# Attention backward with shared K and V heads on one core: whole-batch transfers in ten row slots, and a new order of all units

## The chip, the cores and the metric

One core of a Trainium2 chip runs the kernel alone. The metric is the device time of one execution in microseconds (us). Engines: PE does matrix products and transposes, ACT, DVE and POOL work on tiles, SP issues all the transfers of this kernel, and 16 DMA engines move the bytes. Tiles lie in SBUF with 128 partitions; PE writes to PSUM, here 8 banks of 128 x 512 fp32.

## The reference

Forward attention and its gradients for 32 batches, 32 query heads with 4 query rows each, 4 K/V heads of 2048 rows, head size 128, all in bf16. Eight query heads share one K/V head, so a batch has 4 groups of 32 query rows, 128 rows in all. Per batch:

```
S = q k^T * scale          P = softmax(S)           O = P v
dV = P^T dO                dP = dO v^T              dS = P * (dP - rowsum(O * dO))
dQ = dS k * scale          dK = dS^T q * scale
```

Outputs are O, dQ, dK and dV. q, dO, O and dQ are 32 KB per batch each; K, V, dK and dV are 2 MB per batch each, so a batch moves about 8.5 MB and the whole call 272.65 MB.

## The kernel before, in words

The host lays K and V out as rows: partition p of a batch holds, for each head, 2048 bf16 values. A pair of heads is one row of 4096 values (8192 B, `ROW`). The first pair's K row carries q behind it and the second pair's carries dO (4224 values, 8448 B, `LONG`); dV's and dK's second rows carry O and dQ in the same way. So a batch is loaded with four transfers of 128 rows, about 1 MB each (LK0, LK1, LV0, LV1; line 226), and stored with four (SV0, SV1, SK0, SK1; line 320). `SLOTS = 20` row buffers in SBUF hold loads and results alike: a slot goes from a loaded row to a result row and back. Batch 0 is loaded in halves of a row.

There is no loop over batches that fixes the order. The string `PLAN` lists every unit of work of all batches in the order in which it is emitted, four characters each: the unit's name (through `NAMES`), its part, where it goes (a PSUM bank, an engine A or D, or a slot) and a buffer number. `plan()` reads it, `emit(u)` writes the unit's instructions. Each engine runs its own units in that order; semaphores are set where one unit needs another's data or buffer.

The units of a batch b, with their lines:

- KT, VT (241): one half of one head's K or V block transposed on PE, as fp32 pairs, 4 transposes of 128 x 128 into one bank; KTe, VTe (207 on ACT, 209 on DVE) copy the bank to SBUF. QT and QTe do the same for q and dO.
- S (255): scores, 2 x 8 products into banks 4 to 7. MX (260): negated maximum on DVE. EX (264): exponential on ACT, with its sum. RC, dop, qp, rs: the reciprocal of the sum and dO and q scaled by it.
- ET, ETe, O, Oe (241, 288, 296): the exponentials transposed, O, and O scaled. DL (299): rowsum of O and dO.
- DV, DVe (310, 316): dV in eight parts of 128 x 1024, each evicted as bf16 into a result row by ACT or DVE.
- DP (255), DS (303): dP and dS in two halves. DT, DTe, DQ, DQe: dS transposed, dQ, and dQ scaled. DK, DKe (310, 316): dK in eight parts like dV.

From batch 10 or so the order repeats every batch. Beside batch b's softmax, O and dV stand the K transposes of batch b+1 and the rest of dQ and dK of batch b-1; O of b and dQ of b-1 stand close together. SP's part of a period is SK0(b-1), LV1(b+2), LK0(b+3), SK1(b-1), SV1(b), LV0(b+2), SV0(b), LK1(b+3). SP runs its transfers in that order and waits at each for its slot and its data.

Of the kernel before, what the change touches and what calls it, by code (L numbers as in the profile page):

```python
# [16 lines left out]
ROW = 2 * 16 * P  # L17
LONG = ROW + P
BANKS = 8
SLOTS, E_TILES, DS_TILES = 20, 2, 2  # L20
# [8 lines left out]
    "a000a110b120a030b040a150e400f4A0e011f0A0e702f7A0e513f5A0b160a070e224f2A0e135f1D0c000d0D0e316f3A0g720h7A0e637f6A0"  # L29
    "b080a190g601h6D0g212h2A0i040i1-0j0D0g303h3A0e411f4A0e024f0A0g104h1D0k0A0g415h4D0g026h0D0l0D0e705f7A0e516p020q0A0"  # L30
    "f5D0b1a0p131q1D0m0-0A340B3A0A060B0D0A100B1A0a0d0r020r1-0s0D0t0D0o0-0A640B6A0A760B7D0u020v0D0g502h5A0A540B5A0E1c0"
    "b0e0A460B4A0e210f2D0e102f1D0c020d0D0e333f3A0A240B2A0E0b0u160v1D0g703h7A0e617f6A0n0-0C020D0D0C140D1A0C360D3D0a1h0"
    "g604h6A0g216h2A0i021i1-0j0D0C200D2A0g360h3A0e470f4A0w100x1A0k0A0g111h1D0g462h4D0g075h0D0C400D4D0w061x0A0l0D0e072"
    "f0A0C620D6A0F0f0C740D7D0e763f7A0e504p010q0A0f5D0b1i0p171q1D0m0-0A320B3A0A040B0D0A100B1A0a040r060r1-0s0D0t0D0A720"
    "B7D0o0-0A640B6A0u061v0D0g500h5A0y010C540D5A0y1-0z0D0F1g0A520B5A0E120b0c0A460e201f2A0B4D0e115f1D0c040d0D0e356f3A0"
    "A220B2A0E0j0u160v1D0g701h7A0e617f6A0n0-0C040D0D0C120D1A0C360D3D0a180g605h6A0g216h2A0i020i1-0j0D0C200D2A0g360h3A0"
    "e471f4A0w101x1A0g112h1D0k0A0g463h4D0g074h0D0C400D4D0w060x0A0l0D0e072f0A0C620D6A0F060C740D7D0e765f7A0e506p010q0A0"
    "f5D0b100p171q1D0m0-0A320B3A0A040B0D0A100B1A0a0g0r060r1-0s0D0t0D0o0-0A620B6A0A740B7D0y070C500D5A0y1-0z0D0F1b0u020"
    "v0D0g560h5A0A540B5A0E1f0b020A400B4D0e270f2A0e163f1A0c020d0D0e334f3D0A240B2A0E010u100v1D0g722h7A0e637f6A0n0-0C060"
    "D0D0C140D1A0C300D3D0a130g624h6A0g236h2A0i041i1-0j0D0C220D2A0g300h3A0C720e410f4A0w100x1A0g111h1D0k0A0g403h4D0g015"  # L40
    "h0D0C440D4A0w001x0D0l0D0D7A0e012f0D0C660D6A0F0a0e743f7D0e504p020q0A0f5D0b150p111q1D0m0-0A340B3A0A060B0D0A120B1A0"
    "a0b0r000r1-0s0D0t0D0o0-0A640B6A0A760B7D0y010C520D5A0y1-0z0D0F1j0u041v0D0g500h5A0A560B5A0E160b0f0A420B4D0e211f2A0"
    "e105f1A0c040d0D0e356f3D0A260B2A0E0e0u120v1D0g711h7A0e607f6A0n0-0C040D0D0C160D1A0C320D3D0a170g615h6A0g206h2A0i040"
    "i1-0j0D0C200D2A0g320h3A0e431f4A0w101x1A0g112h1D0k0A0g423h4D0g034h0D0C400D4D0w020x0A0l0D0e032f0A0C640D6A0F0i0C760"
    "D7D0e725f7A0e506p010q0A0f5D0b190p131q1D0m0-0A340B3A0A060B0D0A100B1A0a0j0r020r1-0s0D0t0D0o0-0A640B6A0A760B7D0y030"
    "C500D5A0y1-0z0D0F110u040v0D0g520h5A0A560B5A0E1a0b060A400B4D0e230f2A0e123f1A0c040d0D0e354f3D0A260B2A0E0c0u100v1D0"
    "g732h7A0e627f6A0n0-0C040D0D0C160D1A0C300D3D0a1h0g634h6A0g226h2A0i041i1-0j0D0C220D2A0g300h3A0e410f4A0w120x1A0g131"
    "h1D0k0A0g403h4D0g015h0D0C420D4D0w001x0A0l0D0e012f0A0C640D6A0F000C760D7D0e703f7A0e514p020q0A0f5D0b1e0p131q1D0m0-0"
    "A340B3A0A060B0D0A100B1A0a010r020r1-0s0D0t0D0o0-0A640B6A0A760B7D0y030C500D5A0y1-0z0D0F1d0u041v0D0g520h5A0A560B5A0"
    "E1i0b0a0A400B4D0e231f2A0e125f1A0c040d0D0e356f3D0A260B2A0E020u100v1D0g731h7A0e627f6A0n0-0C040D0D0C160D1A0C300D3D0"  # L50
    "a180g635h6A0g226h2A0i040i1-0j0D0C220D2A0g300h3A0e411f4A0w121x1A0g132h1D0k0A0g403h4D0g014h0D0C420D4D0w000x0A0l0D0"
    "e012f0A0C640D6A0F050C760D7D0e705f7A0e516p020q0A0f5D0b1f0p131q1D0m0-0A340B3A0A060B0D0A100B1A0a0d0r020r1-0s0D0t0D0"
    "o0-0A640B6A0A760B7D0y030C500D5A0y1-0z0D0F140u040v0D0g520h5A0A560B5A0E100b090A400B4D0e230f2A0e123f1A0c040d0D0e354"
    "f3D0A260B2A0E0c0u100v1D0g732h7A0e627f6A0n0-0C040D0D0C160D1A0C300D3D0a1g0g634h6A0g226h2A0i041i1-0j0D0C220D2A0g300"
    "h3A0e410f4A0w120x1A0g131h1D0k0A0g403h4D0g015h0D0C420D4D0w001x0A0l0D0e012f0A0C640D6A0F0i0C760D7D0e703f7A0e514p020"
    "q0A0f5D0b160p131q1D0m0-0A340B3A0A060B0D0A100B1A0a040r020r1-0s0D0t0D0o0-0A640B6A0A760B7D0y030C500D5A0y1-0z0D0F130"
    "u041v0D0g520h5A0A560B5A0E150b0e0A400B4D0e231f2A0e125f1A0c040d0D0e356f3D0A260B2A0E020u100v1D0g731h7A0e627f6A0n0-0"
    "C040D0D0C160D1A0C300D3D0a1b0g635h6A0g226h2A0i040i1-0j0D0C220D2A0g300h3A0e411f4A0w121x1A0g132h1D0k0A0g403h4D0g014"
    "h0D0C420D4D0w000x0A0l0D0e012f0A0C640D6A0F000C760D7D0e705f7A0e516p020q0A0f5D0b1a0p131q1D0m0-0A340B3A0A060B0D0A100"
    "B1A0a030r020r1-0s0D0t0D0o0-0A640B6A0A760B7D0y030C500D5A0y1-0z0D0F170u040v0D0g520h5A0A560B5A0E1i0b0f0A400B4D0e230"  # L60
    "f2A0e123f1A0c040d0D0e354f3D0A260B2A0E0c0u100v1D0g732h7A0e627f6A0n0-0C040D0D0C160D1A0C300D3D0a190g634h6A0g226h2A0"
    "i041i1-0j0D0C220D2A0g300h3A0e410f4A0w120x1A0g131h1D0k0A0g403h4D0g015h0D0C420D4D0w001x0A0l0D0e012f0A0C640D6A0F0h0"
    "C760D7D0e703f7A0e514p020q0A0f5D0b150p131q1D0m0-0A340B3A0A060B0D0A100B1A0a070r020r1-0s0D0t0D0o0-0A640B6A0A760B7D0"
    "y030C500D5A0y1-0z0D0F1j0u041v0D0g520h5A0A560B5A0E100b060A400B4D0e231f2A0e125f1A0c040d0D0e356f3D0A260B2A0E020u100"
    "v1D0g731h7A0e627f6A0n0-0C040D0D0C160D1A0C300D3D0a1e0g635h6A0g226h2A0i040i1-0j0D0C220D2A0g300h3A0e411f4A0w121x1A0"
    "g132h1D0k0A0g403h4D0g014h0D0C420D4D0w000x0A0l0D0e012f0A0C640D6A0F010C760D7D0e705f7A0e516p020q0A0f5D0b1i0p131q1D0"
    "m0-0A340B3A0A060B0D0A100B1A0a0j0r020r1-0s0D0t0D0o0-0A640B6A0A760B7D0y030C500D5A0y1-0z0D0F180u040v0D0g520h5A0A560"
    "B5A0E1h0b0a0A400B4D0e230f2A0e123f1A0c040d0D0e354f3D0A260B2A0E0c0u100v1D0g732h7A0e627f6A0n0-0C040D0D0C160D1A0C300"
    "D3D0a1f0g634h6A0g226h2A0i041i1-0j0D0C220D2A0g300h3A0e410f4A0w120x1A0g131h1D0k0A0g403h4D0g015h0D0C420D4D0w001x0A0"
    "l0D0e012f0A0C640D6A0F0d0C760D7D0e703f7A0e514p020q0A0f5D0b100p131q1D0m0-0A340B3A0A060B0D0A100B1A0a080r020r1-0s0D0"  # L70
    "t0D0o0-0A640B6A0A760B7D0y030C500D5A0y1-0z0D0F1g0u041v0D0g520h5A0A560B5A0E110b050A400B4D0e231f2A0e125f1A0c040d0D0"
    "e356f3D0A260B2A0E020u100v1D0g731h7A0e627f6A0n0-0C040D0D0C160D1A0C300D3D0a160g635h6A0g226h2A0i040i1-0j0D0C220D2A0"
    "g300h3A0e411f4A0w121x1A0g132h1D0k0A0g403h4D0g014h0D0C420D4D0w000x0A0l0D0e012f0A0C640D6A0F040C760D7D0e705f7A0e516"
    "p020q0A0f5D0b1h0p131q1D0m0-0A340B3A0A060B0D0A100B1A0a0g0r020r1-0s0D0t0D0o0-0A640B6A0A760B7D0y030C500D5A0y1-0z0D0"
    "F1b0u040v0D0g520h5A0A560B5A0E1d0b0i0A400B4D0e230f2A0e123f1A0c040d0D0e354f3D0A260B2A0E0c0u100v1D0g732h7A0e627f6A0"
    "n0-0C040D0D0C160D1A0C300D3D0a1a0g634h6A0g226h2A0i041i1-0j0D0C220D2A0g300h3A0e410f4A0w120x1A0g131h1D0k0A0g403h4D0"
    "g015h0D0C420D4D0w001x0A0l0D0e012f0A0C640D6A0F030C760D7D0e703f7A0e514p020q0A0f5D0b110p131q1D0m0-0A340B3A0A060B0D0"
    "A100B1A0a0b0r020r1-0s0D0t0D0o0-0A640B6A0A760B7D0y030C500D5A0y1-0z0D0F190u041v0D0g520h5A0A560B5A0E140b000A400B4D0"
    "e231f2A0e125f1A0c040d0D0e356f3D0A260B2A0E020u100v1D0g731h7A0e627f6A0n0-0C040D0D0C160D1A0C300D3D0a150g635h6A0g226"
    "h2A0i040i1-0j0D0C220D2A0g300h3A0e411f4A0w121x1A0g132h1D0k0A0g403h4D0g014h0D0C420D4D0w000x0A0l0D0e012f0A0C640D6A0"  # L80
    "F070C760D7D0e705f7A0e516p020q0A0f5D0b1d0p131q1D0m0-0A340B3A0A060B0D0A100B1A0a090r020r1-0s0D0t0D0o0-0A640B6A0A760"
    "B7D0y030C500D5A0y1-0z0D0F1e0u040v0D0g520h5A0A560B5A0E130b0h0A400B4D0e230f2A0e123f1A0c040d0D0e354f3D0A260B2A0E0c0"
    "u100v1D0g732h7A0e627f6A0n0-0C040D0D0C160D1A0C300D3D0a1i0g634h6A0g226h2A0i041i1-0j0D0C220D2A0g300h3A0e410f4A0w120"
    "x1A0g131h1D0k0A0g403h4D0g015h0D0C420D4D0w001x0A0l0D0e012f0A0C640D6A0F0f0C760D7D0e703f7A0e514p020q0A0f5D0b140p131"
# [64 lines left out]
def plan():  # L149
    text, seen, units = "".join(PLAN), collections.Counter(), []  # L150
    for at in range(0, len(text), 4):
        key = text[at:at + 2]
        u = Unit()
        u.name, u.part, u.b = NAMES[key[0]], int(key[1]), seen[key]
        u.where, u.tile = text[at + 2], int(text[at + 3], 36)
        seen[key] += 1
        units.append(u)
# [204 lines left out]
```

## Time and profile before

| what | value |
|---|---|
| timed runs | 671.26, 671.86, 672.22 us; median 671.86 us |
| the profiled execution: span from first to last instruction | 671.1 us |
| median of the timed runs less that span | 0.76 us |
| mean granted PE clock | 0.982 |
| HBM read, written | 136.31, 136.31 MB |
| 1024 KB loads of V, 1056 KB loads of K: median from issue to landing | 20.5, 18.1 us |
| stores of 1056 and 1024 KB: median from issue to landing | 20.1, 20.4 us |
| chain of waits by engine | DMA 50%, PE 37%, DVE 4%, ACT 4%, issue 3% |

How to read the profile. Busy time is given for each engine, with its share of the span. Further rows cut the span into 40 equal slices of 16.8 us: digits are tenths of a slice, PEclk is the clock that PE was granted, and the GB/s row tells what the DMA engines moved. A packet is what one DMA engine moves at a time; here one row of a transfer is one packet. The queue q1 carries the kernel's transfers, q8 and q14 those of instructions. The chain of waits goes back from the last instruction to what released it, step by step; a table by stage gives every engine's busy time in a stretch that one chooses.

### The profile page before, as it was taken

To read this page: it belongs to the slowest core of one execution; us is meant where nothing else is said; L and a number is where in the kernel's file an instruction comes from. 1 tells how busy PE (TensorE), PEld (TensorE's weight loads), DVE (VectorE), ACT (ScalarE), POOL (GpSimd) and SP (SyncE) were. 2 spreads that over 40 slices of the span, in tenths; PEclk is the share of its full clock that TensorE was granted. 3 is DMA by queue.
4 is the path that set the end of the run, shared out by engine and by line. 5 is a ranking of instruction groups with operands and counts; after the bars stand their busy time and mean duration, and the time that the engine had idled before them with its cause. 6 is when DMAs were issued, how large, how long until landed. Compare 5 with 4: busy or idle time off the path is not lost.

```text
span 671.1 us, 20678 instructions
## 1 busy us (share of the span) xinstructions
PE 607.9 (91%) x8768; PEld 401.4 (60%) x8768; DVE 572.0 (85%) x736; ACT 569.6 (85%) x802; POOL 39.0 (6%) x102
## 2 busy tenths in 40 slices
PE   6998999999998999988998989988999989898993
PEld 5665566666665666655655655655655666565651
DVE  1988799999997999988888989887888979896994
ACT  4997899999997999888888989887888979886894
POOL 0000000000000000000000000000000000000000
PEclk9999999999998999999999999998999989998997
DMA  9999999999999999999999999999999999999867
GB/s 354 417 424 423 419 381 423 423 423 423 423 426 424 424 423 424 424 425 426 414 420 425 413 417 421 414 422 424 396 388 408 417 424 424 404 421 423 347 258 322
DMA packets 37533, 273.97 MB, mean 408 GB/s; under 512 B 4160, under 2 KB 4160, under 8 KB 5184
## 3 DMA queue, kind: packets, MB, share of 16 engines
q1 hardware_dynamic: 37440, 272.65, 98.2%
q8 instruction: 69, 1.13, 0.6%
q14 instruction: 24, 0.20, 0.1%
HBM read 136.31 MB, written 136.31 MB: 406 GB/s over the span
## 4 chain that ended last, share of the span: by engine, by line
DMA 50%; PE 37%; DVE 4%; ACT 4%; issue 3%; SPq 0%; POOL 0%; DVEq 0%; ACTq 0%; POOLq 0%
DMA row<-in_k_dram 50%; PE psum L241 19%; PE psum L310 8%; PE psum L288 5%; PE psum L255 5%; ACT row L316 3%; DVE vt_sb L209 2%; DVE ds_sb L303 1%; DVE row L316 0%; DVE e_sb L260 0%; ACT e_sb L264 0%; PE psum L230 0%; SPq L226 0%; ACT dt_sb L207 0%; DVE row L296 0%
## 5 line engine op out<-in xcount | busy, mean ns | idle before, releaser
L241 PE MATMUL psum<-ident,row 128*128 128x128 f32 x2048 | 290.1, 284 | 28.4 <-DMA row<-in_k_dram 21.5
L316 ACT CAST row<-psum 128x1024 bf16<-128x1024 f32 x292 | 289.2, 1023 | 30.9 <-PE psum L310 29.1
L241 PEld LDWEIGHTS psum<-ident,row 128*128 128x128 f32 x2048 | 224.7, 143 | 94.8 <-issue 32.0
L316 DVE CAST row<-psum 128x1024 bf16<-128x1024 f32 x220 | 264.9, 1217 | 5.7 <-PE psum L310 2.9
L207 ACT COPY kt_sb<-psum 128x512 f32<-128x512 f32 x190 | 110.2, 598 | 20.6 <-PE psum L241 20.4
L207 ACT COPY vt_sb<-psum 128x512 f32<-128x512 f32 x160 | 92.0, 602 | 35.3 <-PE psum L241 34.6
L303 DVE SCALAR_TENSOR_TENSOR ds_sb<-psum,delta,e_sb 128x1024 bf16<-128x1024 f32 x64 | 82.1, 1283 | 13.4 <-PE psum L255 9.0
L310 PE MATMUL psum<-ds_sb,qp_sb 32*128 32x512 bf16 x512 | 76.9, 383 | 3.4 <-ACT row L316 1.0
L260 DVE TENSOR_SCALAR_CACHE_REDUCE e_sb<-psum 128x2048 bf16<-128x2048 f32 x32 | 73.3, 2292 | 5.7 <-PE psum L255 5.7
L310 PE MATMUL psum<-e_sb,dop_sb 32*128 32x512 bf16 x512 | 68.8, 388 | 2.5 <-issue 1.0
L209 DVE COPY kt_sb<-psum 128x1024 bf16<-128x1024 bf16 x66 | 45.0, 685 | 28.4 <-PE psum L241 27.8
L209 DVE COPY vt_sb<-psum 128x1024 bf16<-128x1024 bf16 x96 | 60.7, 684 | 10.0 <-PE psum L241 9.8
L264 ACT ACTIVATE e_sb<-psum,m 128x2048 bf16<-128x2048 f32 x32 | 64.0, 2001 | 0.2 <-DVE e_sb L260 0.2
L271 POOL TENSOR_SCALAR dop_sb<-row,rinv 128x128 bf16<-128x128 bf16 x32 | 19.3, 603 | 605.3 <-DVE rinv L268 530.3
L241 PE MATMUL psum<-ident,ds_sb 128*128 128x128 f32 x256 | 41.8, 286 | 9.6 <-DVE vt_sb L209 7.0
L288 PE MATMUL psum<-row,dt_sb 128*32 128x128 bf16 x2048 | 43.5, 222 | 6.2 <-issue 5.6
L310 PEld LDWEIGHTS <-qp_sb 32*128 32x128 bf16 x512 | 19.4, 91 | 46.1 <-issue 42.6
L255 PE MATMUL psum<-vt_sb,qdt_sb 128*32 128x512 bf16 x512 | 40.7, 388 | 4.6 <-issue 4.5
L288 PEld LDWEIGHTS <-dt_sb 128*32 128x32 bf16 x2048 | 30.8, 95 | 22.0 <-issue 21.1
L241 PEld LDWEIGHTS psum<-ident,ds_sb 128*128 128x128 f32 x256 | 26.9, 140 | 27.2 <-DVE vt_sb L209 16.4
L207 ACT COPY dt_sb<-psum 128x512 f32<-128x512 f32 x63 | 38.4, 611 | 1.0 <-PE psum L241 0.9
L288 PEld LDWEIGHTS <-et_sb 128*32 128x32 bf16 x2048 | 30.4, 95 | 13.8 <-ACT et_sb L207 11.3
(29 smaller groups left out, 310.1 us busy)
## 6 DMA issues: line engine op xcount, KB each, us to landing
out_dram<-row SPq DMA_DIRECT2D x64, 1056.0 KB, 20.1
out_dram<-row SPq DMA_DIRECT2D x64, 1024.0 KB, 20.4
row<-in_k_dram SPq DMA_DIRECT2D x62, 1056.0 KB, 18.1
row<-in_v_dram SPq DMA_DIRECT2D x62, 1024.0 KB, 20.5
row<-in_v_dram SPq DMA_DIRECT2D x4, 512.0 KB, 9.4
row<-in_k_dram SPq DMA_DIRECT2D x2, 544.0 KB, 5.3
row<-in_k_dram SPq DMA_DIRECT2D x2, 512.0 KB, 4.4
```

Of the source, the lines that this page charges most:

```text
L207: nc.scalar.copy(out=out.bitcast(FP32), in_=in_)
L209: nc.vector.tensor_copy(out=out, in_=in_.bitcast(BF16))
L241: nc.tensor.transpose(out=ps[:, P * j:P * j + P], in_=src[:, 4 * half + j, :], identity=ident32[:])
L255: nc.tensor.matmul(out[r, QW * w:QW * w + QW], lhsT=t["qdt"][:, P * side + 32 * h:P * side + 32 * h + 32], rhs=t[x, NH * i + h][:, QW * w: ...
L260: nc.vector.tensor_scalar(out=t["e"][:], in0=t["S"], scalar1=-scale, scalar2=None, op0=ALU.mult, op1=ALU.min, accum_out=t["m"][:])
L264: nc.scalar.activation(out=t["e"][:], in_=t["S"], func=ACT.Exp, bias=t["m"][:], scale=scale, accum_out=t["l"][:])
L271: nc.gpsimd.tensor_scalar(out=t["dop"][:], in0=t["go"], scalar1=t["rinv"][:], scalar2=None, op0=ALU.mult)
L288: nc.tensor.matmul(t[name][r, :], lhsT=left[:, j, r, odd], rhs=right[:, 4 * i + j, :, odd], start=(i == 0 and c == 0), stop=(i == 1 and c ...
L303: nc.vector.scalar_tensor_tensor(out=t["ds"][:, w], in0=t["DP", i], scalar=t["dl"][:], in1=t["e"][:, w], op0=ALU.subtract, op1=ALU.mult)
L310: nc.tensor.matmul(acc[:, QW * (h % 2):QW * (h % 2) + QW], lhsT=t[still][rows[h], :], rhs=t[moving][rows[h], QW * i:QW * i + QW], start=Tr ...
L316: copy(out=heads_of(t[name[:2], "out", g])[:, :, QW * i:QW * i + QW], in_=t[name[:2], i, g].rearrange("p (h c) -> p h c", h=2))
```

## The change

Rows become whole batches. K, V, dK and dV of a batch are one transfer each: 128 rows of 16384 B, K with q and dO behind it (16896 B), dK and dV with dQ and O behind them (16640 B). Ten slots of 16896 B replace twenty of 8448 B; the bytes in SBUF are the same. Batch 0's K and V are loaded in four pieces, and batch 31's dV and dK are stored in two. The host packs accordingly.

`PLAN` is written anew: the same kinds of units and the same work, in another order. SP's part of a period is SK(b-2), LV(b+2), LK(b+3), SV(b). The rest of a period in the new order, cut to the units about O and dQ:

```
before: ... DV1(b) O(b) Oe DL DV6 DV7 DQ(b-1) DK5(b-1) DQe DP0(b) DS0 VT5 DV5 ... DP1(b) DS1 ...
after:  ... DV3(b) O(b) Oe DV7 DV1 DV6 KT5(b+1) DV5 VT5(b) DK5(b-1) DL DP0(b) DQ(b-1) DV2 DV4 ... DP1(b) DQe DS1 ...
```

In a period the PSUM evictions of line 316 go from 9 on ACT and 7 on DVE to 10 and 6; the copies of KT, VT, ET and DT from 14 on ACT and 6 on DVE to 13 and 7; DQe goes from DVE to ACT. In the repeating part V(b+2) takes the slot that dV(b-1) had, K(b+3) that of V(b), dV(b+1) that of dK(b-2), and dK(b) that of K(b-1).

```diff
-ROW = 2 * 16 * P
-LONG = ROW + P
+ROW = 4 * 16 * P
+OUT, LONG = ROW + P, ROW + 2 * P
...
-SLOTS, E_TILES, DS_TILES = 20, 2, 2
+SLOTS, E_TILES, DS_TILES = 10, 2, 2
+WHOLE = 9
...
-            x = slots[int(u.where, 36)]
-            for h in range(2):
-                t[name[1], 2 * i + h] = x[:, Sk * h:Sk * h + Sk]
+            x, n, src = slots[int(u.where, 36)], *((LONG, k_r) if name == "LK" else (ROW, v_r))
+            for h in range(NH):
+                t[name[1], h] = x[:, Sk * h:Sk * h + Sk]
             if name == "LK":
-                t["q" if i == 0 else "go"] = x[:, ROW:LONG]
-            n = LONG if name == "LK" else ROW
-            src = (k_r if name == "LK" else v_r)[i][b]
-            for w in (slice(0, Sk), slice(Sk, n)) if b == 0 else (slice(0, n),):
-                nc.sync.dma_start(out=x[:, w], in_=src[:, w])
+                t["q"], t["go"] = x[:, ROW:ROW + P], x[:, ROW + P:LONG]
+            cuts = [0, n] if i == WHOLE else [2 * Sk * i, 2 * Sk * i + Sk, n if i else 2 * Sk]
+            for w in map(slice, cuts, cuts[1:]):
+                nc.sync.dma_start(out=x[:, w], in_=src[b][:, w])
...
-            n = LONG if i else ROW
-            nc.sync.dma_start(out=(dv_r if name == "SV" else dk_r)[i][b], in_=t["D" + name[1], "out", i][:, 0:n])
+            w = slice(0 if i in (0, WHOLE) else ROW // 2, OUT if i else ROW // 2)
+            nc.sync.dma_start(out=(dv_r if name == "SV" else dk_r)[b][:, w], in_=t["D" + name[1], "out"][:, w])
```

## The prediction

> **What bounds the kernel now.** I read the page's DMA rows first, since the sum of traffic is fixed, then the table by stage, then the chain of waits, then SP's own queue.
>
> ```profile
> span 671.1 us, 20678 instructions
> PE 607.9 (91%) x8768; PEld 401.4 (60%) x8768; DVE 572.0 (85%) x736; ACT 569.6 (85%) x802; POOL 39.0 (6%) x102
> ...
> DMA  9999999999999999999999999999999999999867
> GB/s 354 417 424 423 419 381 423 423 423 423 423 426 424 424 423 424 424 425 426 414 420 425 413 417 421 414 422 424 396 388 408 417 424 424 404 421 423 347 258 322
> DMA packets 37533, 273.97 MB, mean 408 GB/s; under 512 B 4160, under 2 KB 4160, under 8 KB 5184
> ...
> q1 hardware_dynamic: 37440, 272.65, 98.2%
> q8 instruction: 69, 1.13, 0.6%
> ```
>
> The 16 DMA engines are full in 37 of 40 slices, at about 424 GB/s; only the last three (from 620 us on) are open. 272.65 MB at 424 GB/s are 643 us of the 671.1. Of the rest, the last slices and a few slow ones (381, 396, 388) hold nearly all. The 4160 packets under 512 B are 260 DMAs times 16 engines: each DMA ends with one 4-byte packet on each engine. The table by stage (stretch: length, busy time of PE, PEld, DVE, ACT, POOL, clock, DMA share, GB/s):
>
> ```profile
> 121.85:140.70 18.85, 18.50 (x279) 12.21 (x282) 17.84 (x24) 17.54 (x26) 1.20 (x3) 1.00 1.01 425
> ```
> ```profile
> 399.60:420.10 20.50, 18.60 (x274) 12.29 (x274) 17.99 (x24) 17.71 (x25) 1.29 (x5) 1.00 1.01 421
> ```
> ```profile
> 631.25:671.10 39.85, 28.52 (x515) 16.48 (x513) 28.25 (x36) 29.11 (x39) 1.39 (x4) 0.91 0.71 289
> ```
>
> The first two are one batch each. Early, compute runs a batch in 18.85 us, PE busy for 18.5 of them, and eats the lead that the first loads gave it; later a batch takes 20.5 us with PE idle for 1.9: there the DMA queue paces it. The chain of waits says the same in time order: from 255 us to 606 us it is nearly all DMA, in pieces of one batch.
>
> ```profile
> 399.63 20.42 DMA row<-in_k_dram
> 420.12 20.46 DMA row<-in_k_dram
> ```
>
> The third stretch is the tail. The last load has landed, only stores are left, each waits for compute, and the engines are busy for 0.71 of it: 39.85 x 0.71 = 28.3 us. About 1.55 us lie after the last packet, so some **10.0 us are gaps** in which the queue had nothing to send.
>
> **The price of a row.** The trace keeps a record of each packet. Medians on one engine: 4096 B 159 ns, 4352 B 168, 8192 B 309, 8448 B 319, the 4-byte packet 9. In the full stretches each starts 3 to 4 ns before the last one's recorded end, so consecutive DMAs land 1.25 us apart (512 KB), 2.45 (1024 KB) and 2.53 (1056 KB). Two landings of 512 KB are 2.50 us, one of 1024 KB is 2.45: merging two DMAs into one with rows twice as long saved about 0.047 us (unrounded). By the recorded durations without the overlap it is 2 x 159 - 309 = 9 ns a row, for 8 rows an engine, and one 9 ns packet: 0.081 us.
>
> **The change, part by part.**
>
> 1. Transfers. Bytes stay the same (K rows 16896 B, V 16384, dK and dV 16640). 260 DMAs become 134: 126 x 0.047 = 5.9 us less of full DMA time; by the other count 126 x 0.081 = 10.2. No q1 row is that long, so from the other side: the nearest row of that size is the instruction page, 69 packets of 16 KB in 0.6% of 16 x 671.1 us, some 934 ns each. It shares its engine with q1; less one row of 309 ns between, 625 ns, against 2 x 305.8 = 611.6 for two rows now. 32 batches x 4 tensors x 8 rows = 1024 rows an engine x 13.4 ns is 13.7 us more. So -10.2 to +13.7; I take -5.9, because the four q1 sizes lie on one line and are the nearer rows.
>
> 2. The tail. Before, SP has issued the last load at 619 us and 11 stores follow it, most waiting for data. After, the last load (V of batch 31) stands behind the store of dK(27); after it come dV(29), dK(28), dV(30), dK(29), dV(31), dK(30), dK(31), seven transfers of 4.93 us. Let x be the moment at which dK(26) lands and releases the slot for dV(29), 0.41 of the way through batch 29's units. From x the queue holds five more transfers, 24.6 us, then the seven, 34.5 us: full until x + 59. Compute, no longer held, starts the scores of batch 31 1.59 batches later, x + 30.5 at 19.2 us a batch, and by the trace of before the last eviction is 20.5 us behind those: x + 51. The last store of dK (in two halves) has its place from x + 54. dV(31)'s first half is ready about x + 44, its place x + 44.3; dK(30) x + 46, place x + 47. So the queue stays fed, with 0 to 3 us to spare: of the 10.0 us of gaps I keep 1, bounds 0 and 5. **-9.0 us.**
>
> 3. The start. K(1) whole now precedes the lower half of V(0), which lands about 2.4 us later (18.2 us, not 15.7). The transposes that need it are after the first exponential, which ends at 19.7 in the trace of before; so 0 to 2 us for compute, and nothing for the queue: six loads fill it until 33 us, and the dV(0) store that is next needs dV(0), ready at 28.3 before. Cover gone, that wait would be a gap of as much.
>
> 4. The slots. Ten whole ones replace twenty halves, the same memory, freed later. In the period SP issues dK(b-2), V(b+2), K(b+3), dV(b). V(b+2) goes where dV(b-1) was, so SP is held until that store lands, with K(b+3), dV(b) and dK(b-1) queued behind it in that order. Cover: the store of dK(b-2), 4.93 us. K(b+3) waits for the last read of V(b), at 0.62 of batch b, over a batch earlier. dV(b+1) goes where dK(b-2) was: that landing is now what holds compute. Semaphore waits on landings were there before too (SP, for its DMAs' landings, in the waits view), so I cost these at 0; what they cost uncovered is the slower rival below.
>
> 5. The order of the units. PE does the same work, 18.5 us a batch. Per batch ACT gets one PSUM eviction more (+1.02), one 128x512 copy less (-0.60) and the scaling of dQ (0.35): 17.5 to 18.3. DVE goes from 17.8 to 17.0. Score matmuls (1.05), minimum (2.29), exponential (2.00) and their hand-overs make a chain of 5.9 us; in it the new order gives PE those matmuls (0.9), eight transposed blocks (8 x 0.43) and a dK pair (0.3): 4.7. So PE may wait 1.2 us: 18.85 at best, 18.5 + 1.2 = 19.7 at worst; placing the units one after the other with these durations I get 19.2. All are under the queue's 20.3, so the order costs 0. It decides only from 19.9 on: the scores of batch 1 start at 30.4 us and those of batch 31 28.6 us before the end (chain of waits), so 30.4 + 30 x 19.9 + 28.6 = 656.
>
> **Sum.** 671.1 - 5.9 - 9.0 = 656.2 of span. The median of the runs shown (671.86) is 0.76 above the span, so 657.0. Counting up from packets instead (2 us before the first, 632 us of rows, 12.4 us by which packets ran over their medians, 4.7 us of instruction fetch, 1.6 us at the end, 1 of gaps, 0.8) gives 654.5. I take **656.0**.
>
> Two rules weighed. The trace's landings, 2.45 us apart for 1024 KB, hold no fixed cost beyond the 0.047 above. The Trainium skill's DMA: Bandwidth & Descriptors (Anatomy of one DMA) gives about 2.0 us fixed plus bytes over 436 GB/s for each DMA; 126 fewer would then be 252 us, an estimate, if none of it were hidden; eight DMAs in flight (20 us to land, 2.5 apart) hide it here. The same page (Queues, rings and completion order) speaks against the change: an engine drains a whole packet of one queue before it turns to another, so an instruction page would wait behind rows of 0.61 us (by the line through the sizes above), not 0.31. An estimate by it is 69 x 0.3 = 21 us if every page stalled an engine; the chain of waits has 3% of issue time in all, and that is covered while the queue paces.
>
> **Rivals.**
> - Compute paces (chance 0.12). The new order runs at 20.0 to 20.3 us a batch, because ACT at 18.3 and PE at 18.5 get in each other's way. For it: PE is busy for 18.5 of 18.85 already. Against: the sums in 5. 30.4 + 30 x 20.15 + 28.6 = 663.5; 659 to 668.
> - The long rows bring nothing or cost (0.08). Rows at 625 ns: +13.7 instead of -5.9, and the tail as forecast: 671.1 + 13.7 - 9.0 + 0.8 = 676.6 at the far end, 663 with no gain at all. For it: the only 16 KB packets are slow; against: those share their engine.
> - Slower: SP starves the queue (0.10). At each V load SP waits for a landing with one transfer, 4.93 us, as cover. The landing is that of the slowest engine (one DMA's landings are up to 2.5 us apart here), then an issue (0.34 us) and about 1.0 us from issue to packet, as at the start: 3.9 us. From 4.93 on it decides. Past it by 1.0 us for 28 batches: 656 + 28 = 684. At 0.6 us it is 673. For it: eight DMAs in flight become two at that moment; against: 1.0 us of margin.
> - The forecast: the queue full from 2 us to nearly the end, 650 to 660 (0.70).
>
> The range takes the forecast, compute pacing and the rows without gain: 648 to 669, leaving the 684 and 677 cases and a run that loses the slow packets too (about 0.17). Under 0.2% (1.3 us) can't be told from no change here. Faster 0.84, within 0.2% 0.03, slower 0.13.
>
> **What would show it.** q1 with 19552 packets, 2144 under 512 B; middle slices at 427 to 429 GB/s; a batch of the paced part at about 20.2 us; DMA digits at 9 to the last slice or two. Median issue to landing: V loads near 10 us, K 15, dV 20, dK 25. Records of 16384 B near 609 ns; 625 would be the second rival. DMA digits of 7 or 8 in the middle would be starving; PE at 9 throughout with the DMA open, compute pacing. A tail at 0.7 of DMA share would prove step 2 wrong.

## The result, and the profile after

The changed kernel is slower: 688.71 us median (four runs, 686.49 to 688.98) against 672.04 for the kernel before (four runs beside it). The ratio is 1.0241, 95% interval 1.0224 to 1.0258. The forecast was 656.0, faster. The rival that gave the slower side, "SP starves the queue", had a chance of 0.10, and 684 us at 1.0 us a batch. The median is 2.5 us above the profiled span; the prediction had added 0.8.

The page of the changed kernel, rows that answer to those of before:

```profile
span 686.2 us, 20449 instructions
...
DMA  9999999999999999999999999999999999999996
GB/s 362 419 426 426 426 426 357 409 409 382 430 424 423 400 390 388 393 371 408 397 405 398 391 429 380 398 389 406 414 394 400 411 392 406 387 401 407 378 422 289
DMA packets 19674, 273.93 MB, mean 399 GB/s; under 512 B 2176, under 2 KB 2176, under 8 KB 3200
...
q1 hardware_dynamic: 19584, 272.64, 97.9%
```

Every DMA digit is a 9, to the last slice but one: the tail is as full as forecast. But a full digit isn't a full rate. From the 14th slice on (223 us) the queue moves mostly 370 to 414 GB/s where 427 to 429 were forecast. I had named digits of 7 or 8 in the middle as the sign of starving, and this page has none; the sign stands one row lower. The table by stage shows it more sharply (stretch: length, busy time of PE, PEld, DVE, ACT, POOL, clock, DMA share, GB/s). First the changed kernel:

```profile
275.50:295.14 19.64, 19.12 (x276) 12.68 (x275) 17.10 (x22) 18.41 (x27) 1.20 (x3) 1.00 1.00 399
441.00:462.70 21.70, 21.11 (x300) 13.62 (x298) 18.29 (x24) 20.41 (x30) 1.20 (x3) 1.00 0.99 393
517.20:521.00 3.80, 3.61 (x88) 2.23 (x88) 3.57 (x6) 3.80 (x6) 0.00 (x0) 1.00 1.02 322
646.40:686.20 39.80, 24.96 (x354) 14.79 (x354) 21.72 (x26) 24.52 (x33) 1.21 (x3) 0.79 0.87 366
```

In all four stretches the engines are busy for 0.87 to 1.02 of the time, yet 322 to 399 GB/s come out: packets take longer than their medians. The third stretch is the second half of one K load. The chain of waits in the middle is made of pieces that end in stores, not in K loads as before (start, length, what):

```profile
530.87 25.57 DMA out_dram<-row
...
573.43 20.75 DMA out_dram<-row
595.59 25.11 DMA out_dram<-row
```

And SP's own waits name the wait that the change added. The first line is the load's wait for a store in the kernel before (line 226); the other two are the changed kernel's (line 217 is the load, line 311 the store):

```profile
SPq L226 <- DMA out_dram<-row: 105.4, 23, 5.6
```

```profile
SPq L217 <- DMA out_dram<-row: 449.3, 27, 19.9
SPq L311 <- DVE row L307: 79.1, 12, 19.1
```

For 449 us, in 27 pieces, SP stands at a load (nearly always V's) and waits for a store to land; before it was 105 us in 23 pieces. The median times from issue to landing came out as forecast for the loads (10, 15 us):

```profile
out_dram<-row SPq DMA_DIRECT2D x62, 2080.0 KB, 20.7
row<-in_k_dram SPq DMA_DIRECT2D x31, 2112.0 KB, 15.6
row<-in_v_dram SPq DMA_DIRECT2D x31, 2048.0 KB, 10.3
```

V's 10.3 us is V itself and one store: a queue two transfers deep, as the slots prescribe.

**Where the time went.** The records of the packets give a sum that closes for every kernel of this study. On one engine, from its first packet to its last: all rows at the median of their size, less the 3 to 4 ns by which each packet starts before the recorded end of the last; plus what packets ran over that median (overrun), plus gaps between packets. In us, means over 16 engines; 2 us lie before the first packet and 3 to 5 behind the last:

```
kernel          span   rows   overrun  gaps   of the gaps, after 600 us
before          671.1  637.6   13.2    15.3   10.4
after           686.2  632.3   35.5    11.8    1.4
```

So the long rows saved 5.3 us and the fuller tail 9.0, both as forecast. Overrun cost 22.3, and gaps ahead of 600 us rose from 4.9 to 10.4. By size, the overrun is 19.8 us in K rows, 11.2 in V rows and 3.8 in stores. By place in the transfer, where an engine moves eight rows, counted 0 to 7, K's sits in rows 4 to 7 (17.8 us), and V's in its first row (7.1), the one behind the wait.

### The profile page after: what moved, and what is told of

Its sections match the earlier page's. It is cut to its first block, busy times and chain, and to the rows that moved or that the text cites. A ratio compares the mean times of both kernels' runs of the same rounds, so it can differ in the third digit from the quotient of the medians.

```text
span 686.2 us, 20449 instructions
## 1 busy us (share of the span) xinstructions
PE 626.5 (91%) x8768; PEld 414.6 (60%) x8768; DVE 552.8 (81%) x712; ACT 588.6 (86%) x826; POOL 39.3 (6%) x102
## 4 chain that ended last, share of the span: by engine, by line
PE 39%; DMA 33%; ACT 18%; issue 5%; DVE 3%; SPq 1%; ACTq 0%; DVEq 0%
DMA out_dram<-row 31%; PE psum L232 18%; PE psum L301 10%; ACT row L307 9%; PE psum L279 6%; ACT vt_sb L199 4%; PE psum L246 4%; ACT e_sb L255 3%; ACT kt_sb L199 2%; DMA row<-in_k_dram 2%; DVE row L307 1%; SPq L217 1%; PE psum L221 1%; DVE e_sb L251 1%; DVE vt_sb L201 1%
## 5 line engine op out<-in xcount | busy, mean ns | idle before, releaser
L307 ACT CAST row<-psum 128x1024 bf16<-128x1024 f32 x318 | 317.7, 1020 | 51.5 <-DMA out_dram<-row 25.9
L307 DVE CAST row<-psum 128x1024 bf16<-128x1024 f32 x194 | 236.4, 1219 | 36.4 <-DMA out_dram<-row 19.4
L199 ACT COPY kt_sb<-psum 128x512 f32<-128x512 f32 x160 | 95.2, 596 | 16.8 <-PE psum L232 14.8
L301 PE MATMUL psum<-e_sb,dop_sb 32*128 32x512 bf16 x512 | 80.9, 385 | 22.4 <-ACT row L307 21.6
L294 DVE SCALAR_TENSOR_TENSOR ds_sb<-psum,delta,e_sb 128x1024 bf16<-128x1024 f32 x64 | 82.1, 1284 | 15.6 <-PE psum L246 11.6
L251 DVE TENSOR_SCALAR_CACHE_REDUCE e_sb<-psum 128x2048 bf16<-128x2048 f32 x32 | 73.3, 2291 | 24.8 <-PE psum L246 24.0
L201 DVE COPY kt_sb<-psum 128x1024 bf16<-128x1024 bf16 x96 | 65.9, 688 | 33.7 <-PE psum L232 33.4
L201 DVE COPY vt_sb<-psum 128x1024 bf16<-128x1024 bf16 x97 | 66.0, 683 | 4.0 <-PE psum L232 1.7
L301 PEld LDWEIGHTS <-dop_sb 32*128 32x128 bf16 x512 | 24.9, 91 | 54.2 <-issue 38.5
L279 PEld LDWEIGHTS <-dt_sb 128*32 128x32 bf16 x2048 | 35.6, 100 | 17.9 <-issue 12.4
L246 PEld LDWEIGHTS <-qdt_sb 128*32 128x32 bf16 x1024 | 21.5, 94 | 37.0 <-issue 32.4
L246 PE MATMUL psum<-kt_sb,qdt_sb 128*32 128x512 bf16 x512 | 38.3, 382 | 2.8 <-ACT row L307 0.7
## 6 DMA issues: line engine op xcount, KB each, us to landing
row<-in_v_dram SPq DMA_DIRECT2D x31, 2048.0 KB, 10.3
row<-in_v_dram SPq DMA_DIRECT2D x4, 512.0 KB, 10.5
```

The lines of the kernel that those rows point to most:

```text
L199: nc.scalar.copy(out=out.bitcast(FP32), in_=in_)
L201: nc.vector.tensor_copy(out=out, in_=in_.bitcast(BF16))
L246: nc.tensor.matmul(out[r, QW * w:QW * w + QW], lhsT=t["qdt"][:, P * side + 32 * h:P * side + 32 * h + 32], rhs=t[x, NH * i + h][:, QW * w: ...
L251: nc.vector.tensor_scalar(out=t["e"][:], in0=t["S"], scalar1=-scale, scalar2=None, op0=ALU.mult, op1=ALU.min, accum_out=t["m"][:])
L279: nc.tensor.matmul(t[name][r, :], lhsT=left[:, j, r, odd], rhs=right[:, 4 * i + j, :, odd], start=(i == 0 and c == 0), stop=(i == 1 and c ...
L294: nc.vector.scalar_tensor_tensor(out=t["ds"][:, w], in0=t["DP", i], scalar=t["dl"][:], in1=t["e"][:, w], op0=ALU.subtract, op1=ALU.mult)
```

## The experiments

Three theories. Theory 1: the wait for the landing of dV(b-1) with one store as cover leaves too little in the queue, and the loads behind it run over. Theory 2: rows of 16 KB are slow in themselves. Theory 3: the loads are slow because K and V run back to back, or because of compute beside them.

### The V load behind the K load

```
 # units = plan()
+    for b in range(10, 32):
+        v, k = (next(u for u in units if (u.name, u.b) == x) for x in (("LV", b), ("LK", b + 1)) if x[1] < 32) if b < 31 else (None, None)
+        if v is not None:
+            units.remove(v)
+            units.insert(units.index(k) + 1, v)
```

> The kernel after, but from batch 10 on the load of V(b+2) is issued behind that of K(b+3) instead of ahead of it, so that the wait for the landing of dV(b-1) has two transfers as cover (dK(b-2) and K(b+3), some 9.9 us) and not one (4.93). Theory 1, starving: the engines run dry at that wait, start again together, and the loads behind it run over their medians; with the second cover all of this goes. 655 to 664 us, a paced batch 20.2 to 20.5 us instead of 21.5, middle slices at 424 GB/s or more. Theory 2, rows of 16 KB are slow in themselves: 685 to 690, as after. Theory 3, the loads are slow because K and V now run back to back or because of what compute does beside them, and only the idle time comes from the wait: the excess of the K rows (18 us) stays, the first row of V (7 us) gets well: 675 to 682.

Measured: 670.46 us, ratio to the kernel before 0.9972 (0.9953 to 0.9991). That is 18 us below the change as it was made, by the place of one instruction in SP's order, and level with the kernel before (0.3% below it). Its stages:

```profile
275.59:295.25 19.66, 19.13 (x276) 12.69 (x275) 17.11 (x22) 18.43 (x27) 1.21 (x3) 1.00 1.01 427
577.67:597.99 20.32, 19.17 (x276) 12.72 (x275) 17.01 (x23) 18.43 (x27) 1.20 (x3) 1.00 1.01 424
629.00:668.85 39.85, 27.99 (x438) 16.65 (x436) 24.72 (x31) 27.73 (x37) 1.20 (x3) 0.84 0.86 359
```

The first stretch is the same batch as the first of the changed kernel above, with the same engines busy for the same time and the DMA share the same: 427 GB/s instead of 399. The second is a batch that the queue paces: 20.32 us, where theory 1 and the prediction had 20.2 to 20.5. K's overrun fell from 19.8 to 3.9 us. Theory 2 is out, and so is the half of theory 3 that blames compute for K. The time itself missed its range of 655 to 664 by 6 us: gaps from 60 to 200 us are still 3.6, the tail has 6.2 again, and V, now the last load ahead of a store, has 10.0 us of overrun, most of it in rows 4 to 7.

### Half rows

```
-            cuts = [0, n] if i == WHOLE else [2 * Sk * i, 2 * Sk * i + Sk, n if i else 2 * Sk]
+            cuts = [0, 2 * Sk, n] if i == WHOLE else [2 * Sk * i, 2 * Sk * i + Sk, n if i else 2 * Sk]
...
-            w = slice(0 if i in (0, WHOLE) else ROW // 2, OUT if i else ROW // 2)
-            nc.sync.dma_start(out=(dv_r if name == "SV" else dk_r)[b][:, w], in_=t["D" + name[1], "out"][:, w])
+            cuts = [0, ROW // 2, OUT] if i == WHOLE else [0, ROW // 2] if i == 0 else [ROW // 2, OUT]
+            for w in map(slice, cuts, cuts[1:]):
+                nc.sync.dma_start(out=(dv_r if name == "SV" else dk_r)[b][:, w], in_=t["D" + name[1], "out"][:, w])
```

> The kernel after in its order and its slots, but every transfer of a batch issued as two, back to back, each of half a row (8192 B and what follows it). Theory 1, starving: the wait for dV(b-1) still has one store as cover, in two halves now: 684 to 696 us, about 400 GB/s in the middle. Theory 2, rows of 16 KB are slow in themselves: the rate of before returns, 424 GB/s, with the full tail of after: 660 to 668. Theory 3, back-to-back loads or compute beside them: as theory 1, 684 to 696.

Measured: 677.83 us, 1.0081 (1.0049 to 1.0113): between the theories, a miss for each. Overrun is 21.1 us, gaps 11.6, and the rows cost 5.1 us more than whole ones. Halves change the wait too: V's first half needs only the first half of the store to land, so it has 7.4 us of cover, not 4.9. The copies below take that apart.

### The transfers alone

Six copies have no compute at all. Their loop is all there is (the one shown has one store as cover):

```
K_SLOTS, V_SLOTS = 7, 3        # free-running copy: 6, 4
for b in range(B + 2):
    for name, at in (("SK", b - 2), ("LV", b + 2), ("LK", b + 3), ("SV", b)):
        move(name, at)         # slot of K(b): b % K_SLOTS, of V(b): b % V_SLOTS
```

> Transfers alone, no compute: the loads and stores of after in its order and with its rows, dK stored from K's slot and dV from V's, so that the output is not the reference's. Six slots for K and four for V: SP's waits for landings all have four or more transfers as cover. Theory 1: rows of 16 KB run at 427 to 429 GB/s, 272.65 MB in 640 to 646 us. Theory 2, the rows are slow: 400 GB/s, 680 us or more. Theory 3, if back-to-back loads are what slows: 665 to 680; if it is compute beside them: 640 to 646.

Measured: 643.57 us, span 641.8.

> The same transfers alone, no compute, output not the reference's, with seven slots for K and three for V: V(b+2) goes where dV(b-1) was, so that SP is held at each V load with one store, 4.93 us, as cover, as in the kernel after, but here from the first batches on. Theory 1: a batch takes 21.3 to 21.7 us instead of 20.1, 675 to 690 us in all, V's first row and the middle rows of K run over their medians. Theory 2, the rows are slow in themselves: as the copy without that wait. Theory 3, compute beside the loads is what slows them: only the idle time is seen, 0.3 us a batch and V's first rows, 650 to 665.

Measured: 677.1 us, span 675.3. The two pages, free-running first:

```profile
DMA  8999999999999999999999999999999999999996
GB/s 363 430 414 433 429 430 431 428 430 430 430 430 430 431 433 428 431 431 430 431 431 431 429 432 432 430 431 429 432 432 431 432 431 431 433 430 432 431 431 276
```

```profile
DMA  9989999999999999999999999999999999999998
GB/s 366 431 333 413 431 428 428 422 407 390 403 398 416 396 389 391 405 425 427 422 411 411 404 422 389 403 393 396 413 395 408 391 405 390 401 403 400 399 433 361
```

Same bytes, same order, same rows; one slot less for V, one more for K. 430 GB/s becomes 390 to 410 for most of the run, with digits of 9 in both. So rows of 16 KB are not slow, and the slot alone costs 33.5 us without any compute: theory 1, and the loss of the changed kernel in small. Little of it is idle time (5.4 us more gaps):

```
copy                             span   rows   overrun  gaps
free-running                     641.8  632.0    2.4     0.1
one store as cover               675.3  632.0   33.4     5.5
two transfers as cover           645.1  632.0    4.1     2.7
halves, V lower half first       646.8  637.5    3.3     0.3
halves, V upper half first       661.1  637.4   15.2     3.4
one load as cover                677.7  632.0   33.4     8.7
```

Not one store packet ran over in the copies with whole rows. In the copy with one store as cover 24.5 of the 33.4 us are in K rows, 8.9 in V rows.

```
-    for name, at in (("SK", b - 2), ("LV", b + 2), ("LK", b + 3), ("SV", b)):
+    for name, at in (("SK", b - 2), ("LK", b + 3), ("LV", b + 2), ("SV", b)):
```

> The copy whose V load goes where dV(b-1) was (seven slots for K, three for V), with K(b+3) issued ahead of V(b+2): the same wait, with two transfers (9.9 us) as cover. No compute; the output is not the reference's. If running dry is what made the loads of the copy with one store as cover slow (675.3 us of span against 641.8), all of it goes: 641 to 647. If any wait of SP for a landing costs, whatever its cover: 655 or more.

Measured: 646.84 us, span 645.1. The same wait for the same landing, with 9.9 us of cover, costs 3 us in 31 batches. So a wait for a landing costs next to nothing here when enough stands in the queue.

```
-        cuts = [0, n]
+        cuts = [0, ROW // 2, n]
```

> The copy with one store as cover again, every transfer as two DMAs of half rows (8192 B and what follows). No compute; the output is not the reference's. If the loads run slow because the engines start together after the wait, whatever the rows: 668 to 680, as with whole rows (675.3). If it takes rows of 16 KB after such a start: 648 to 658, the idle time (5 us) and 4 us for more packets being left.

Measured: 648.59 us, span 646.8. By itself this spoke for the length of the rows; but the first half has 7.4 us of cover, so the order of V's halves was turned:

```
-        for w in map(slice, cuts, cuts[1:]):
+        for w in list(map(slice, cuts, cuts[1:]))[::-1 if name == "LV" else 1]:
```

> The copy in half rows and with three V slots again, with the two halves of each V load in reversed order (upper half first). The first of them waits for the upper half of the store of dV(b-1), which lands last: the cover is 4.9 us again (two halves of dK(b-2)) and not some 7.4 as in the halves before. No compute; the output is not the reference's. If the cover decides, whatever the rows: 665 to 680, like whole rows (675.3). If rows of 16 KB are needed for the slow loads: 647 to 655, near the other copy in halves (646.8).

Measured: 662.87 us, span 661.1: neither number. With the cover at 4.9 us again, 14.3 us come back, so cover decides whether there is a loss. At the same 4.9 us half rows lose 15.2 us of overrun where whole rows lose 33.4, but this does not show that long rows are dearer in a shallow queue. In this copy the sixteen landings of the store ahead of V's load are 0.4 to 0.9 us apart up to 163 us, in whole rows 2.4 us by 126 us; so, worked out from the landings, V's load is issued less than 2 us ahead of its first packet in 12 of 28 batches here, and in 23 of 28 there. Where it is under 1.5 us a batch loses much the same: 1.2 to 1.5 us (three batches in half rows), 1.1 to 1.6 (14 in whole rows). Between 1.5 and 2 us it is 0.7 and 1.0 in the mean. Long rows cost nothing in a deep queue; whether their length adds to the price of a shallow one stays open.

```
-    for name, at in (("SK", b - 2), ("LV", b + 2), ("LK", b + 3), ("SV", b)):
+    for name, at in (("SK", b - 2), ("SV", b - 1), ("LK", b + 3), ("LV", b + 2)):
```

> The copy in whole rows with three V slots, the period ordered dK(b-2), dV(b-1), K(b+3), V(b+2): V's load still goes where dV(b-1) was and is still held with one transfer (4.9 us) as cover, but that transfer is now K's load, and what runs behind the wait is one load and then stores, not two loads. No compute; the output is not the reference's. The copy with two loads behind the wait lost 33.5 us of span against the free one (641.8), 24.5 of it in the K rows that run 5 to 11 us after the start, in the last load ahead of a store. If the loss belongs to the last load ahead of a store, wherever the wait stands: 665 to 680, now in V's rows. If it takes two loads in a row behind a dry queue: 645 to 655, the idle time and V's first rows being left.

Measured: 679.48 us, span 677.7. Here K is the cover, one load runs behind the wait, and 32.4 of 33.4 us are in V, 24.0 of them in its rows 4 to 7; K has 1.0. The overrun belongs to the last load ahead of a store. Two loads in a row are not needed, and the rest of theory 3 falls.

**What the cover has to cover.** The copy with one store as cover has batches with and without the loss. Its packet records, batch by batch from 60 us on, sort by one number: the time from the issue of V's load to the first V packet on the engine that gets there first.

```
issue to first packet   batches   overrun of the K load behind it, ns on a mean engine
2.5 us and more            3        3 to 36
2.0 to 2.3 us              2      107 to 180
1.0 to 1.95 us            22      609 to 1291 (mean 1007)
```

Call this time the lead. It is the cover less the spread of the store's landings less SP's reaction: in this copy the landings grow apart from 1.0 us at 83 us to 2.5 at 124, and the lead falls from 3.4 to 1.95. In the copy with two transfers as cover the lead is 2.6 to 7.5 us in 27 batches, and V, there the last load, has 1 to 136 ns; its last load has a lead of 0.98, and 1754. In the changed kernel 19 of the 23 V loads that are issued from 120 us on with a K load behind them have a lead of 0.99 to 1.7 us, and K 329 to 1172 ns (mean 884).

So the loss begins before the queue is empty: in this copy, when a load is issued less than about 2 us ahead of its turn. That edge is not sharp and not the same everywhere: with one load as cover, V's loads with leads of 2.0 to 2.7 us still have 144 to 533 ns. Nor must it be a load that waits: at 109 and 152 us of the changed kernel a store is issued late, for want of its data, 0.85 us ahead of its first packet, and the K load behind it has 1216 and 1100 ns. Why a late issue slows rows that run 5 to 11 us later is not settled; no run here shows the mechanism. A burst of four issues does not do it by itself: the copy with two transfers as cover issues four in 2.8 us, if not as fast as the copy with one store (1.4 us).

### The order of the units by itself

```
+            if i == WHOLE and u.where in full:
+                cuts = [n - THIN, n]
+            full.add(u.where)
...
-            w = slice(0 if i in (0, WHOLE) else ROW // 2, OUT if i else ROW // 2)
+            w = slice(OUT - THIN, OUT) if i == WHOLE else slice(ROW // 2 * i, ROW // 2 * i + THIN)
```

> The kernel after with its compute, order and slots, but after the first load into each slot the loads, and all stores, move only the last 1024 of some 8300 columns of each row, so that the queue is never full. The output is not the reference's; compute works on what was left in the slots. It shows what the order of the units takes by itself. As the prediction had it: 19.2 us a batch, 14 + 16 + 30 x 19.2 + 28.6 = 635 us. By the batches of the kernel after that no transfer held (19.65 us, first scores at 33.4, 30.5 behind the last): 33.4 + 30 x 19.65 + 30.5 = 653 us, so that compute alone is as long as the transfers alone, and every hold of either shows in the sum.

> The kernel before in the same way: its compute, order and slots, with loads (after the first into each slot) and stores cut to the last 512 columns of each half row; the output is not the reference's. By its fastest batches: 31.5 + 30 x 18.85 + 27.5 = 625 us, against 653 (or 635, as the prediction had it) for the order of after. If the slots or SP's order hold compute in it too, 632 or more.

Measured: 653.6 us (span 651.8) for the new order and 627.14 (span 625.3) for the old one. One batch of each, new order first:

```profile
293.61:313.25 19.64, 19.12 (x276) 12.71 (x275) 17.01 (x23) 18.43 (x27) 1.20 (x3) 1.00 0.17 55
```

```profile
263.30:282.14 18.84, 18.48 (x276) 12.20 (x274) 17.85 (x24) 17.55 (x25) 1.20 (x3) 1.00 0.19 57
```

Both came out as the batches of the whole kernels had it (653 and 625), not as the prediction had the new order (635). With the queue open, the new order takes 0.80 us more a batch, 0.64 of it PE's busy time (19.12 against 18.48, for the same 276 instructions; why was not taken apart). Alone it needs 651.8 us, 10 more than the transfers alone (641.8), where the old order had 16 to spare.

### Both orders with two transfers as cover

```
-SP, a period: SK(b-2), LV(b+2), LK(b+3), SV(b);  V(b+2) where dV(b-1) was
+SP, a period: SV(b), LV(b+3), SK(b), LK(b+4);    K(b+4) where dV(b) was, V(b+4) where dK(b) was,
+                                                 dV(b) where V(b-1) was, dK(b) where K(b-1) was
```

Shown for the old order; for the new one the stores come in the order in which their data are ready, and loads alternate with them in the same way.

> The whole-batch transfers of after with the compute order of before (its units word for word, only loads and stores replaced). SP alternates: store, load, store, load; each load takes the slot of the store two places ahead of it, so two transfers (9.9 us) cover every wait for a landing; dK(b) goes where K(b-1) was and dV(b) where V(b-1) was, so that no result waits for a landing. If the loss of after was the one-transfer cover and an order of units that is itself as long as the transfers (651.8 us alone against 625.3 for that of before): queue full from 2 us to the last batches, 643 to 655 us. If whole-batch slots are too coarse for this compute, whatever the order, or SP's single queue holds stores behind loads: 662 to 675.

> The same transfers, slots and alternation, with the compute order of after. If the order of the units is the second half of the loss: compute alone takes 651.8, so 654 to 664 us, 8 to 14 us more than the run with the order of before, and less than the 670.5 of the swapped V load, since here every wait is covered from the first batch on. If the order costs nothing, as the prediction had it: the same as the run with the order of before, within 3 us.

Measured: 672.33 us with the old order, 1.0001 (0.9977 to 1.0026), and 675.75 with the new one, 1.0053 (1.0034 to 1.0071). Both missed. The order of the units is worth 3.4 us between the medians, not 8 to 14, and single runs of the old order lie between 668.2 and 675.7. And whole transfers with two transfers as cover and the old order are as fast as the kernel before, not 17 to 29 us faster. Two stages of the run with the old order:

```profile
263.00:282.00 19.00, 18.65 (x294) 12.37 (x294) 17.84 (x26) 17.71 (x26) 1.20 (x3) 1.00 1.01 426
630.00:670.36 40.36, 28.66 (x372) 16.30 (x372) 24.45 (x28) 24.97 (x33) 1.20 (x3) 0.75 0.67 280
```

The middle runs at 426 GB/s, but the tail is open again: 280 GB/s. Seven stores are left when the last load has landed, as in the changed kernel, but PE had waited for that batch's K (19.5 us of waits for K loads in the run, batch 31 takes 24.8 us), so the stores aren't ready. Its sum is rows 632.3, overrun 17.9, gaps 15.8, of which 11.2 after 600 us; for the new order 632.3, 20.1, 16.6 and 9.0.

And the waits did not stay covered. In the run with the old order the sixteen landings of one transfer are under 2 us apart at 60 us and 7 to 8 us from 300 us on. Of 9.9 us of cover that leaves about 2: from 283 us on every load of this run is issued only 1.6 to 2.4 us ahead of its first packet. Loads with a lead under 2.5 us hold 9.5 of the 17.9 us of overrun, with the new order 10.5 of 20.1. So these two runs don't price the order, or whole-batch slots, with every wait covered; that is untested.

## Why the prediction was wrong, point by point

The forecast's span was 656.2; the changed kernel's is 686.2, 30.0 more.

- **Transfers (step 1), right.** -5.9 forecast; rows at their medians went from 637.6 to 632.3, -5.3. The two copies that lose least give 5.0 (646.8 less 641.8, halves against whole). The rows stayed on the line: 16384 B have a median of 611 ns, against 609 forecast. The other count, -10.2, and 625 ns are out: instruction pages have a median of 941 ns before and 949 after, with rows twice as long beside them, which speaks against a row of the kernel's being part of the 934 ns. There are 136 DMAs, not the 134 that I counted.
- **Tail (step 2), right in size, but it hung on step 4.** Gaps after 600 us went from 10.4 to 1.4, the 9.0 that were forecast. (One reading was off: at 631 us of the kernel before the last load had not landed. Its sixteen landings run from 626.6 to 640.1 us.) The swapped kernel has the same last transfers but for the swap, and 6.2; the covered old order has 11.2. The tail of the changed kernel was full because the queue came late to it and compute had its results waiting. "From x the queue holds five more transfers" is a statement about which of the two is behind, and step 4 had that wrong.
- **Start (step 3), right for its stretch.** Gaps up to 60 us: 0.3, before 0.5. From 60 to 200 us they grew from 1.4 to 3.3, SP standing at stores whose data came late (79.1 us on line 307 in its waits over the whole run). The prediction has no term for that.
- **Slots (step 4), the step that failed.** "Semaphore waits on landings were there before too ..., so I cost these at 0." Uncovered, they cost most of the 22.3 us of overrun (16.7 went with the swap) and 3.7 us of gaps between 200 and 600 us. The rival had the mechanism, the place and nearly the time (684), and I priced it out with "From 4.93 on it decides", 3.9 us being used. That its 684 came so near is in part luck: it priced idle time, 28 us of it, and the gaps ahead of 600 us grew by 5.5; the rest of the loss is overrun. Issue and first packet were about right: 0.43 us from the last landing to the issue and 1.0 from there to a packet at 167 us of the copy with one store as cover (0.34 and 1.0 forecast).

  Two things were not. The first is the spread. "One DMA's landings are up to 2.5 us apart here" holds in the trace of before only up to about 90 us; they are 3 to 8 us apart by 200 us and 12 to 14 from 300 us on. In the changed kernel those of the store that V's load waits for are 2.9 to 4.4 us apart from 228 us on. So the trace of before already showed that 2.5 us is no bound. The second: the queue doesn't have to be empty, the loss starts at a lead of some 2 us. With 2.9 to 4.4 of spread, 0.43 for the issue and 2 of lead, 5.3 to 6.8 us must be covered, and 4.93 were there. Nor were the waits of before known to be free: worked out from its landings, one K load of each batch from 307 us on was issued 1.2 to 2.3 us ahead of its first packet there too. The price is not idle time either, so it can't be read off by how far past the edge one is: it jumps from some 0.1 to about 1 us a batch.
- **Order (step 5), nearly right, and too cheap.** 19.64 us a batch, inside 18.85 to 19.7 but above the 19.2 that I took. It didn't decide in the changed kernel. It does in the swapped one from 200 to 400 us, where every batch but a few takes 19.65: compute alone at 651.8 us and transfers alone at 641.8 leave no room, so every hold of either shows in the sum. "They cost 0" is true only of a mean over batches.
- **The sign.** I said that digits of 7 or 8 would show starving. The digits stayed 9, since most of the loss is in packets whose records are longer, and a packet's whole record counts as busy.

The Trainium skill's page DMA: Bandwidth & Descriptors (Why a DMA increments its semaphore by 16 and not by 1) says that only the full count of 16 tells that all data has landed; the traces agree, SP issuing 0.43 us after the last 4-byte packet of the sixteen engines, and it is the spread of those sixteen which used up the cover. The same page (Anatomy of one DMA) puts about 2.0 us of fixed cost on each DMA; the section fits that to DMAs which GpSimd issues, and here SP issues all of them, so the prediction's 252 us was no bound for this kernel. The copies measure 0.04 us for each of 128 DMAs saved while the queue is deep (5.0 / 128).

What stays open: how a late issue slows the last load ahead of a store, and why whole kernels keep 13 to 20 us of overrun with two transfers or more as cover, where copies have 2 to 4. About half of it in the two runs with two transfers as cover lies in loads with a lead under 2.5 us, behind engines that land 7 to 8 us apart; in the copies that lose 2 to 4 us they are 5 to 7 us apart in the middle of the run, with 2.6 us of lead or more. Why the engines drift further apart beside compute, and where the other half comes from, no run here took apart.

## What to carry to other kernels

When a transfer goes into a slot that another must leave, count what stands in the queue behind that other one, in us on the engine that runs ahead, and take off the spread of the landings, the issue and some 2 us of lead: one transfer of 4.9 us was not enough here; two were in a copy without compute, and in whole kernels they were soon down to 2 us of lead. The spread has to be read from the landings in the middle of the run, not at its start: it was 0.3 us at the first loads of the kernel before and 14 later. Moving one load behind the next in the issuing engine's order was worth 18 us of 688. Read GB/s beside the busy share of the DMA engines, since a starved queue shows as 9s at a lower rate. When two resources take nearly the same time alone (652 and 642 us here), measure each alone before adding up savings: what is gained in one place, such as the tail, is given back where the other falls behind.

## What the runs showed of the hardware

- A DMA queue whose engines are hardly ever idle can lose 7% of its rate: 400 GB/s over 84 us from 400 us on instead of 432 over 80 us, in two copies with the same packets that differ in when loads are issued (length, busy time of DVE and POOL, clock, DMA share, GB/s):

```profile
400.00:484.00 84.00, 0.00 (x0) 0.00 (x0) 1.00 1.00 400
```

```profile
400.00:480.00 80.00, 0.00 (x0) 0.00 (x0) 1.00 1.01 432
```

- In the copies the overrun sits mostly in rows 4 to 7 (of 0 to 7) of the last load ahead of a store (22 of 24.5 us, and 24 of 32.4 when the other load is last). Stores in whole rows show none.
- The 16 engines drift apart: in the free-running copy their landings of one load are 0.8 us apart at the start and 5.4 us from 380 us on, and what overrun there was (22 to 108 ns a K load between 14 and 206 us) goes to near zero on the way. A wait for the slowest engine once a batch doesn't by itself set this back: with two transfers as cover the landings go from 0.9 to 6.9 us apart, with one store as cover they stay at 2.0 to 3.8 from 120 us on. In the kernel before they reach 14.
- At 4.9 us of cover, 8 KB rows lost 15.2 us and 16 KB rows 33.4; by the leads above, most of that is in how many batches came short, not in the rows.
